# Attention pairs of a fused kernel: the last score tile and the denominators in the bank of the one-chunk values, and three pieces of work elsewhere in the queues

## The chip, the cores and the metric

The kernel runs on one core of a Trainium2 chip. The metric is the device time of one execution in microseconds (us), here the median of three runs. The core's engines are TensorE (PE, with its weight loads shown as PEld), VectorE (DVE), ScalarE (ACT), GpSimd (POOL) and SyncE (SP), which issues most DMA transfers. Each engine works through its own queue in the order in which the program was written; engines wait for each other by semaphores. PSUM, into which TensorE writes, has eight banks of 512 fp32 columns on 128 partitions.

## What is computed

Three layers in a row: attention with rotary embedding over 4 batches and 8 heads of 576 tokens with 64 dimensions, a dense block `h - tanh(h)`, and a block that sends chosen tokens to one of 8 experts. The change lies in the attention:

```python
q_rot, k_rot = (rotate(q), rotate(k))
scores = scale * np.matmul(q_rot, k_rot.transpose(0, 1, 3, 2))
scores = scores - np.max(scores, axis=-1, keepdims=True)
attn = np.exp(scores)
attn = attn / (np.sum(attn, axis=-1, keepdims=True) + 1e-09)
return np.matmul(attn, v).astype(np.float32)
```

## The kernel before

**Work.** The 32 heads are taken as 16 pairs (`p`). A head's 576 rows are four and a half chunks of 128; the two halves left over share one mixed chunk, so that a pair has 9 chunks, numbered 0 to 8, chunk 4 being the mixed one. Every number is fp32; a matmul of two fp32 operands is three matmuls of rounded high and low parts (`high`, `low`).

**Steps.** The loop in `attention` goes over pairs and, in each, over five steps `s` (`STEPS`): steps 0 to 3 take two chunks, step 4 the mixed chunk alone. A step writes the scores of its chunks into score banks ("pair" tiles, two of two banks each; `scores`, L229), has VectorE take the negated row max (`nm`, L234), has ScalarE take the exponent with the row sum beside it (`exponent`, L247), and has TensorE transpose finished exponents in tiles of 128x128 (`transpose`, L261). A pair has 41 tiles. Chunk `c` owns the tiles from `FIRST[c]` on; tiles 36 to 40 are those of the mixed chunk. `BEFORE[s]` and `BEHIND[s]` list the tiles transposed ahead of and behind a step's scores; those in `BEHIND[0]`, 36 to 40, belong to the pair that has just ended and are done in step 0 of the next one.

**Banks of the tiles.** Four tiles fill a bank. Banks 0 and 1 are taken in turn (`cnt["b"]`), so that a pair takes eleven: ten full ones and one for tile 40, into which the transposed denominators (9 rows of 128 columns) go as well. `evacuate` copies full banks to the tile `eT` in SBUF (L271), on ScalarE, but for the bank of tiles 36 to 39, which VectorE copies. Banks 2 and 3 hold the values: bank 2 those of the eight whole chunks, bank 3, in its first 64 columns, those of the mixed chunk (`values`, `pav`). The score tiles take the other four.

**Step 0 of pair p.** In order: `evacuate` (tiles 28 to 35 of p - 1, two ScalarE copies); `denominators(p - 1)`, a ScalarE copy of 9 sums per row with 1e-9 added (L275) and a VectorE reciprocal (L276); `scores`; the transposes of tiles 36 to 40 and of the reciprocals (L263); the copies of the two banks, VectorE and ScalarE; `spread(p - 1)`, a VectorE copy of the transposed reciprocals (`sT`, L281), its transfer to DRAM (L282) and back to all partitions (`rb`, L284 and L285); the exponents; the rotations of pair p + 2 on GpSimd (L201 to L203); and the last part of the values of p - 2 (`AV[3]`, L303). Step 1 ends the pair p - 2 (`finish`, L325 and L328, VectorE), which multiplies the values of both banks by the spread reciprocals, and then starts the values of p - 1 in both.

**Weights on the side.** A 64-bit weight block per pair is decoded to fp32 in four parts (`w_decode`): part 0 on ScalarE (L350), parts 1 to 3 on VectorE (L352 and L354; L357; L362). They stand behind the scores and exponents of the steps in `W_AT` = (1, 2, 4), in pair 0 of `W_AT0` = (3, 4, 4). Part 3 ends a block: most are stored to DRAM at the next step 0 (`w_store`), but in pairs 13 and 14 the block stays, and ScalarE casts its high part (L126) and GpSimd takes the low part (L127) at once.

**After the loop** come the stores, the rest of the values and the first matmuls of the MoE stage (`g1(0, ...)`, L531), between whose halves `last_transposes` ends the last pair.

**Waits within a bank.** The semaphores come from a framework that orders any two accesses of different engines to one PSUM tile, and so to one bank.

Of the kernel before, what the change touches and what calls it, by code (L numbers as in the profile page):

```python
# [19 lines left out]
P = 128  # L20
# [3 lines left out]
NP = 16  # L24
# [20 lines left out]
W_AT, W_AT0 = (1, 2, 4), (3, 4, 4)  # L45
# [5 lines left out]
BEHIND = range(36, 41), range(4, 8), range(12, 18), range(20, 26), range(28, 36)  # L51
# [28 lines left out]
class Chain:  # L80
# [90 lines left out]
    def attention(self, ctx):  # L171
        nc, tc = self.nc, self.tc
        a1 = ctx.enter_context(tc.tile_pool(name="a1", bufs=1))

        def tile_(shape, tag, dt=F32, bufs=1):
            return a1.tile(shape, dt, tag=tag, name=tag, bufs=bufs)
# [36 lines left out]

        cnt = {"b": 0}

        def scores(p, cs):

            (qh, ql), (kh, kl) = parts[p, 0], parts[p, 1]
            banks = [self.pair_bank() for _ in cs]
            for i in range(2):
                for n, (q, k) in enumerate(((qh, kh), (ql, kh), (qh, kl))):
                    for c, sc in zip(cs, banks):
                        r = slice(0, P) if c == 4 else half[c // 5]
                        a = P * (c % 5)
                        x = 288 * i + (0 if c in (1, 3, 6, 8) else 64)
                        nc.tensor.matmul(sc[:, i, :288], q[r, a:a + P], k[r, x:x + 288], start=n == 0, stop=n == 2)  # L229
            if p not in st:  # L230
                st[p] = {"sums": tile_([P, 9], "sums", bufs=2), "eT": tile_([P, 44 * P], "eT", bufs=2)}
            for c, sc in zip(cs, banks):
                nm = tile_([P, 1], "nm", bufs=4)
                nc.vector.tensor_reduce(out=nm, in_=sc[:, :, :288], axis=AX.XY, op=ALU.max, negate=True)  # L234
                st[p][c] = (sc, nm)
# [15 lines left out]
        def transpose(p, tiles):  # L251

            d = st[p]
            for L in tiles:
                c = max((a, c) for c, a in enumerate(FIRST) if a <= L)[1]
                j, odd = L - FIRST[c], c in (1, 3, 6, 8)
                if L % 4 == 0:
                    d["pt"] = self.bank(cnt["b"] % 2)
                    cnt["b"] += 1
                x = 512 * odd + j * P  # L260
                nc.tensor.transpose(d["pt"][:, (L % 4) * P:(L % 4 + 1) * P], d["e", c][:, x:x + P], self.ident)  # L261
                if L == 40:
                    nc.tensor.transpose(d["pt"][:9, P:2 * P], d["s2"], self.ident)  # L263
                if L % 4 == 3 or L == 40:
                    full.append((d, d["pt"], L))

        def evacuate(f=nc.scalar.copy, n=None):
            for _ in range(len(full) if n is None else n):
                d, pt, L = full.pop(0)
                a, n = (L - L % 4) * P, (L % 4 + 1) * P  # L270
                f(d["eT"][:, a:a + n], pt[:, :n])  # L271

        def denominators(p):
            s2 = st[p]["s2"] = tile_([P, 9], "s2", bufs=2)
            nc.scalar.activation(s2, st[p]["sums"], AF.Copy, bias=1e-9)  # L275
            nc.vector.reciprocal(s2, s2)  # L276

        def spread(p):
            d = st[p]
            sT = tile_([9, P], "sT", bufs=2)  # L280
            nc.vector.tensor_copy(sT, d["pt"][:9, P:2 * P])  # L281
            nc.sync.dma_start(self.rd[p].rearrange("(c t) -> c t", t=P), sT)  # L282
            rb = d["rb"] = self.k([P, 1024], "wraw", bufs=4)[:, :SK] if p + 1 == NP else tile_([P, SK], "rb", bufs=2)
            nc.sync.dma_start(rb[:64, 64:], self.rd[p, :S].partition_broadcast(64))  # L284
            nc.sync.dma_start(rb[64:, :S], self.rd[p, S:].partition_broadcast(64))  # L285

        def values(p):
            d = st[p]
# [7 lines left out]
                a = 4 * h + j  # L296
                return eT[:, a:a + 36].rearrange("k (a n) q -> k a n q", a=2)[:, :, 0:10 + h:9 + h]

            d["pav"] = (self.bank(2), self.bank(3))

            def main(j):
                for h in range(2):
# [111 lines left out]
        for p in range(NP):  # L414
            for s, cs in enumerate(STEPS):
                if s:
                    transpose(p, BEFORE[s])
                evacuate()
                for i in range(2):
                    if s == CAST_AT[i] and p + 1 < NP:  # L420
                        high(p + 1, i)
                if s == (MAGNITUDE_AT if p else W_AT0[0]):
                    w_decode(p, 0)
                if s == 0 and p:
                    denominators(p - 1)
                if s == 1 and p > 1:
                    finish(p - 2)
                scores(p, cs)
                if s:
                    transpose(p, BEHIND[s])  # L430
                elif p:
                    transpose(p - 1, BEHIND[0])
                    evacuate(nc.vector.tensor_copy, 1)
                    evacuate()
                    spread(p - 1)
                for c in cs:
                    exponent(p, c)
                if p == 0 and s == 0:
# [10 lines left out]
                    for h in range(2):  # L449
                        nc.sync.dma_start(vt[half[h], 4 + h], self.vr[p])  # L450
                for i, at in enumerate(W_AT if p else W_AT0):
                    if s == at:
                        w_decode(p, i + 1)
                if s == W_LOAD_AT:
                    w_store()
# [18 lines left out]
        def last_transposes():  # L474
            denominators(NP - 1)
            evacuate()
            transpose(NP - 1, BEHIND[0])
            evacuate()
            spread(NP - 1)

        self.g1(0, last_transposes)
        self.load_w(9)
# [1 line left out]
        for f in values(NP - 1):  # L484
            f()
# [866 lines left out]
```

## Time and profile before

| | us |
|---|---|
| median of three runs | 896.14 |
| the runs | 895.75, 901.04, 896.14 |
| the profiled execution | 895.3 |
| its span, first to last instruction | 893.5 |

The mean granted clock of TensorE in the profiled execution is 0.983 of full speed. A row of the timeline has the start in us from the span's start, the duration in us, engine, line, operation, output<-inputs with shapes, and how many instructions were merged; in square brackets stands how long the engine was idle before it, and what ended that. Idle times under some tens of ns are not shown.

### The profile page before, as it was taken

To read this page: it belongs to the slowest core of one execution; us is meant where nothing else is said; L and a number is where in the kernel's file an instruction comes from. 1 tells how busy PE (TensorE), PEld (TensorE's weight loads), DVE (VectorE), ACT (ScalarE), POOL (GpSimd) and SP (SyncE) were. 2 spreads that over 40 slices of the span, in tenths; PEclk is the share of its full clock that TensorE was granted. 3 is DMA by queue.
4 is the path that set the end of the run, shared out by engine and by line. 5 is a ranking of instruction groups with operands and counts; after the bars stand their busy time and mean duration, and the time that the engine had idled before them with its cause. 6 is when DMAs were issued, how large, how long until landed. Compare 5 with 4: busy or idle time off the path is not lost. (4 is left out here: it accounts for less than half of the span.)

```text
span 893.5 us, 14400 instructions
## 1 busy us (share of the span) xinstructions
PE 834.4 (93%) x5224; PEld 678.4 (76%) x5224; DVE 686.7 (77%) x1248; ACT 520.7 (58%) x1064; POOL 297.1 (33%) x190
## 2 busy tenths in 40 slices
PE   4699989999999999999999999999999998899996
PEld 4465656665665579998998898998998887788874
DVE  3788888888887679987877877787887975776571
ACT  3677778877777767554454454544444464355550
POOL 6964575657651100000300200110110246435452
PEclk8799999999999999999999999999999999999998
DMA  8257655675564163230020011002001056497760
GB/s 302 82 194 238 226 194 205 231 256 183 180 220 145 42 246 119 82 106 1 1 91 16 1 61 46 2 14 95 1 1 72 24 201 201 123 335 259 238 218 11
DMA packets 53866, 117.55 MB, mean 132 GB/s; under 512 B 7547, under 2 KB 13195, under 8 KB 53792
## 3 DMA queue, kind: packets, MB, share of 16 engines
q1 hardware_dynamic: 51152, 111.06, 36.4%
q0 software_dynamic: 2640, 5.55, 1.8%
q8 instruction: 42, 0.69, 0.3%
q14 instruction: 32, 0.26, 0.1%
HBM read 92.84 MB, written 24.79 MB: 132 GB/s over the span
## 5 line engine op out<-in xcount | busy, mean ns | idle before, releaser
L234 DVE TENSOR_REDUCE nm<-pair 128x1 f32<-128x576 f32 x144 | 102.0, 744 | 43.7 <-PE pair L229 42.7
L531 PE MATMUL pair<-xh,wh 128*128 128x384 f32 x384 | 131.9, 343 | 0.9 <-DVE ct L587 0.9
L531 PE MATMUL pair<-xh,wl 128*128 128x384 f32 x384 | 129.4, 337 | 0.0
L531 PE MATMUL pair<-xl,wh 128*128 128x384 f32 x384 | 129.2, 336 | 0.0
L596 ACT CAST gh<-cq 128x384 fp32r<-128x384 f32 x96 | 46.7, 512 | 129.6 <-PE bank L545 75.8
L545 PE MATMUL bank<-wh,gl 128*128 128x512 f32 x288 | 112.6, 391 | 0.0
L545 PE MATMUL bank<-wl,gh 128*128 128x512 f32 x288 | 112.5, 391 | 0.0
L545 PE MATMUL bank<-wh,gh 128*128 128x512 f32 x288 | 112.3, 390 | 0.0
L261 PE MATMUL bank<-ident,e 128*128 128x128 f32 x576 | 91.9, 288 | 20.2 <-ACT e L247 11.8
L247 ACT ACTIVATE e<-pair,nm 128x576 f32<-128x576 f32 x128 | 93.7, 738 | 28.8 <-DVE nm L234 27.0
L127 POOL TENSOR_TENSOR xl<-wraw,xh 128x768 fp32r<-128x768 f32 x12 | 23.1, 1924 | 262.1 <-ACT xh L126 262.0
L229 PE MATMUL pair<-k,q 64*128 64x288 f32 (+1 forms) x864 | 97.1, 318 | 12.4 <-ACT emix L247 9.5
L261 PEld LDWEIGHTS bank<-ident,e 128*128 128x128 f32 x576 | 63.1, 143 | 56.2 <-ACT e L247 39.1
L271 ACT COPY eT<-bank 128x512 f32<-128x512 f32 (+1 forms) x161 | 83.3, 555 | 24.6 <-PE bank L263 15.0
L229 PEld LDWEIGHTS pair<-k,q 64*128 64x128 f32 (+1 forms) x864 | 73.1, 190 | 28.8 <-ACT emix L247 12.9
L580 ACT ACTIVATE cu<-pair 128x384 f32<-128x384 f32 x96 | 47.1, 490 | 49.8 <-PE pair L531 49.7
L531 PEld LDWEIGHTS pair<-xh,wh 128*128 128x128 f32 x384 | 72.1, 188 | 4.7 <-issue 1.6
L531 PEld LDWEIGHTS pair<-xl,wh 128*128 128x128 f32 x384 | 72.2, 188 | 1.2
L531 PEld LDWEIGHTS pair<-xh,wl 128*128 128x128 f32 x384 | 72.1, 188 | 0.0
L303 PE MATMUL bank<-eT,vt 128*64 128x512 f32 x256 | 69.8, 624 | 0.0
L594 DVE COPY_PREDICATED cq<-ck,ct 128x384 f32<-128x384 uint8 x96 | 65.1, 678 | 2.8
L927 ACT CAST wh<-wraw 128x1024 fp32r<-128x1024 f32 x56 | 56.6, 1050 | 16.2 <-DMA wraw<-w 16.0
(216 smaller groups left out, 1826.0 us busy)
## 6 DMA issues: line engine op xcount, KB each, us to landing
wraw<-w SPq DMA_DIRECT2D x56, 512.0 KB
raw<-qs SPq DMA_DIRECT2D x15, 640.0 KB
raw<-ks SPq DMA_DIRECT2D x15, 640.0 KB
wu<-w_in SPq DMA_DIRECT2D x8, 1024.0 KB
wu<-w_out SPq DMA_DIRECT2D x8, 1024.0 KB
w_d<-wb SPq DMA_DIRECT2D x14, 512.0 KB
wraw<-w_d SPq DMA_DIRECT2D x14, 512.0 KB
wraw<-xf_d SPq DMA_DIRECT2D x12, 384.0 KB
```

The source lines that it names most:

```text
L229: nc.tensor.matmul(sc[:, i, :288], q[r, a:a + P], k[r, x:x + 288], start=n == 0, stop=n == 2)
L234: nc.vector.tensor_reduce(out=nm, in_=sc[:, :, :288], axis=AX.XY, op=ALU.max, negate=True)
L247: nc.scalar.activation(o.rearrange("p (h s) -> p h s", h=2), sc[:, :, :288], AF.Exp, bias=nm, accum_out=st[p]["sums"][:, c:c + 1])
L261: nc.tensor.transpose(d["pt"][:, (L % 4) * P:(L % 4 + 1) * P], d["e", c][:, x:x + P], self.ident)
L271: f(d["eT"][:, a:a + n], pt[:, :n])
L303: nc.tensor.matmul(d["pav"][0][half[h]], vt[:, j, half[h]], of_head(h, j), start=j == 0, stop=j == 3)
L531: self.nc.tensor.matmul(h[f], a[:, k, fs], b[:, k], start=n == 0, stop=n == 11)
L545: self.nc.tensor.matmul(self.acc[g][t], a[:, f, ts], b[:, f], start=(p == 0 and f == 0 and i == 0), stop=(p == 7 and f == 1 and i == 2))
L580: nc.scalar.activation(u, x, AF.Square)
L594: V.copy_predicated(q, mk, th)
L596: nc.scalar.copy(gh, q)
L927: self.nc.scalar.copy(h, self.eraw[l, q])
```

## The change

Bank 3 becomes one tile, `odds`, for all of the attention: columns 0 to 63 hold the mixed chunk's values as before, columns 128 to 255 tile 40, columns 256 to 383 the transposed denominators. Tile 40 takes no bank of the two alternating ones any more. `last_tiles` transposes the last five tiles, has VectorE copy tiles 36 to 39, calls `spread`, and has VectorE copy tile 40; in the last pair too, where ScalarE made both copies before. `denominators` goes ahead of `evacuate` in step 0. The decode parts that stand at step 4 (part 3; in pair 0 parts 2 and 3) go from behind the step's exponents to ahead of its scores.

```diff
@@ attention @@
         cnt = {"b": 0}
 
+        odds = self.bank(3)
+
@@ transpose @@
-                if L % 4 == 0:
+                if L == 40:
+                    d["pt"] = odds[:, P:2 * P]
+                elif L % 4 == 0:
                     d["pt"] = self.bank(cnt["b"] % 2)
                     cnt["b"] += 1
...
                 if L == 40:
-                    nc.tensor.transpose(d["pt"][:9, P:2 * P], d["s2"], self.ident)
+                    nc.tensor.transpose(odds[:9, 2 * P:3 * P], d["s2"], self.ident)
@@ spread @@
-            nc.vector.tensor_copy(sT, d["pt"][:9, P:2 * P])
+            nc.vector.tensor_copy(sT, odds[:9, 2 * P:3 * P])
...
+        def last_tiles(p):
+
+            transpose(p, BEHIND[0])
+            evacuate(nc.vector.tensor_copy, 1)
+            spread(p)
+            evacuate(nc.vector.tensor_copy, 1)
+
@@ values @@
-            d["pav"] = (self.bank(2), self.bank(3))
+            d["pav"] = (self.bank(2), odds)
@@ the loop over pairs and steps @@
                 if s:
                     transpose(p, BEFORE[s])
+                if s == 0 and p:
+                    denominators(p - 1)
                 evacuate()
...
                 if s == (MAGNITUDE_AT if p else W_AT0[0]):
                     w_decode(p, 0)
-                if s == 0 and p:
-                    denominators(p - 1)
                 if s == 1 and p > 1:
                     finish(p - 2)
+                for i, at in enumerate(W_AT if p else W_AT0):
+                    if s == at == 4:
+                        w_decode(p, i + 1)
                 scores(p, cs)
                 if s:
                     transpose(p, BEHIND[s])
                 elif p:
-                    transpose(p - 1, BEHIND[0])
-                    evacuate(nc.vector.tensor_copy, 1)
-                    evacuate()
-                    spread(p - 1)
+                    last_tiles(p - 1)
...
                 for i, at in enumerate(W_AT if p else W_AT0):
-                    if s == at:
+                    if s == at != 4:
                         w_decode(p, i + 1)
@@ last_transposes @@
             denominators(NP - 1)
             evacuate()
-            transpose(NP - 1, BEHIND[0])
-            evacuate()
-            spread(NP - 1)
+            last_tiles(NP - 1)
```

## Rows read from the trace of the kernel before

**Rows 1.** The page, busy us of each engine (share of the span), instructions

```profile
PE 834.4 (93%) x5224; PEld 678.4 (76%) x5224; DVE 686.7 (77%) x1248; ACT 520.7 (58%) x1064; POOL 297.1 (33%) x190
```

**Rows 2.** Table of stretches, 200 to 250 us: busy us by engine, PEclk, DMA share, GB/s

```profile
200.00:250.00 50.00, 46.29 (x387) 29.77 (x386) 44.31 (x59) 38.53 (x88) 33.70 (x19) 1.00 0.58 196
```

**Rows 3.** Waits of PE, 60 to 300 us: total us, times, longest

```profile
PE bank L261 <- DVE eT L271: 6.4, 13, 0.7
```

**Rows 4.** Timeline, 160 to 182 us, the end of pair 7

```profile
164.15 0.76 DVE L234 TENSOR_REDUCE nm<-pair 128x1 f32<-128x576 f32 x1 [1.38 <-PE pair L229]
...
164.94 0.74 ACT L247 ACTIVATE emix<-pair,nm 128x576 f32<-128x576 f32 x1 [0.28 <-DVE nm L234]
...
165.67 1.07 ACT L271 COPY eT<-bank 128x512 f32<-128x512 f32 x2
...
166.62 0.23 ACT L275 ACTIVATE s<-sums 128x9 f32<-128x9 f32 x1
...
166.81 0.77 PE L261 MATMUL bank<-ident,emix 128*128 128x128 f32 x5
...
167.61 1.08 PE L303 MATMUL bank<-eT,vt 128*64 128x512 f32 x4
167.72 0.27 ACT L271 COPY eT<-bank 128x128 f32<-128x128 f32 x1 [0.87 <-PE bank L263]
167.88 0.75 ACT L247 ACTIVATE e<-pair,nm 128x576 f32<-128x576 f32 x1
...
168.28 0.68 DVE L271 COPY eT<-bank 128x512 f32<-128x512 f32 x1
...
168.88 0.27 DVE L281 COPY sT<-bank 9x128 f32<-9x128 f32 x1
...
169.11 0.63 PE L261 MATMUL bank<-ident,e 128*128 128x128 f32 x4 [0.42 <-DVE eT L271]
...
170.77 1.42 DVE L234 TENSOR_REDUCE nm<-pair 128x1 f32<-128x576 f32 x2 [0.64 <-PE pair L229]
```

**Rows 5.** One line's instructions (ns min/median/max), and a group of POOL, 60 to 300 us

```profile
L362 DVE SCALAR_TENSOR_TENSOR wb<-wu,wb x16: 1214/1756/2580, 36.4 to 311.7; 128x1024 uint32<-128x1024 uint32 x16
...
L201 POOL TENSOR_TENSOR t<-raw,csq 128x640 f32<-128x640 f32 x11 | 20.8, 1895 | 68.5 <-DMA raw<-qs 44.4 <-DVE nm L234 18.0 <-DVE k L212 6.1
```

**Rows 6.** Timeline, 30 to 46 us, the end of pair 0

```profile
34.44 1.88 DVE L357 SCALAR_TENSOR_TENSOR wb<-wu,wb 128x1024 uint32<-128x1024 uint32 x1
...
35.44 1.80 PE L229 MATMUL pair<-k,q 64*128 64x288 f32 x11 [3.29 <-ACT emix L247]
...
36.36 2.46 DVE L362 SCALAR_TENSOR_TENSOR wb<-wu,wb 128x1024 uint32<-128x1024 uint32 x1
...
40.96 1.09 PE L261 MATMUL bank<-ident,e 128*128 128x128 f32 x4 [1.58 <-DVE eT L271]
```

**Rows 7.** Timeline, 53 to 62 us, the end of pair 1

```profile
55.10 2.12 POOL L202 TENSOR_TENSOR t<-raw,csq 128x640 f32<-128x640 f32 x1
...
55.97 0.76 DVE L234 TENSOR_REDUCE nm<-pair 128x1 f32<-128x576 f32 x1
56.64 1.67 DVE L362 SCALAR_TENSOR_TENSOR wb<-wu,wb 128x1024 uint32<-128x1024 uint32 x1
```

**Rows 8.** Timeline, 127 to 130 us, the end of pair 5

```profile
127.68 1.56 POOL L201 TENSOR_TENSOR t<-raw,csq 128x640 f32<-128x640 f32 x1 [6.12 <-DVE k L212]
```

**Rows 9.** Timeline, 272 to 283 us, the end of pair 13

```profile
273.67 0.74 ACT L247 ACTIVATE emix<-pair,nm 128x576 f32<-128x576 f32 x1 [1.00 <-DVE nm L234]
...
274.81 1.05 ACT L126 CAST wh<-wb 128x1024 fp32r<-128x1024 f32 x1 [0.30 <-DVE wb L362]
...
281.47 1.42 DVE L234 TENSOR_REDUCE nm<-pair 128x1 f32<-128x576 f32 x2 [0.85 <-PE pair L229]
```

**Rows 10.** Timeline, 291 to 302 us, the end of pair 14

```profile
293.03 0.74 ACT L247 ACTIVATE emix<-pair,nm 128x576 f32<-128x576 f32 x1 [0.90 <-DVE nm L234]
...
300.20 1.42 DVE L234 TENSOR_REDUCE nm<-pair 128x1 f32<-128x576 f32 x2 [0.64 <-PE pair L229]
```

## The prediction

> **What bounds the kernel now.** I read the page first: TensorE is busy 93% of the span, no other engine over 77% [rows 1]. Then the table of stretches, since the change lies in the attention stage alone (about 16 to 316 us, 16 pairs of some 18 us): in 50 us there TensorE is busy 46.3, VectorE 44.3, ScalarE 38.5 [rows 2]. So TensorE bounds this stage with small holes, and only what closes or opens a hole counts. Then who TensorE waits for between 60 and 300 us: 6.4 us, 13 times, for VectorE's copy at L271 [rows 3]. Last the timeline around the end of a pair, which I call a boundary and number by the pair that ends; number 7 stands for eight that look alike (1, 2, 3, 4, 6, 7, 9, 12) [rows 4]. There the reader is to see: the max of step 4 (164.15, VectorE idle 1.38 before it), the exponent of the mixed chunk (164.94), which frees the score bank that TensorE needs for the next pair; the transposes of the last five tiles (166.81); the values matmuls (167.61 to 168.69); and then 0.42 us of nothing until 169.11, because the first four tiles of the next pair go into the bank whose 512 columns VectorE has just copied out (ends 168.96).
>
> **The change, part by part.**
>
> *Tile 40 and the denominators move to bank 3.* A pair now takes ten banks of the two alternating ones in place of eleven. So the first tiles of the next pair no longer follow tiles 36 to 39 in one bank but tiles 32 to 35, whose copy on ScalarE is over by 166.74 (165.67 + 1.07, plus the 0.23 below) [rows 4]. The wait of 6.4 us in 13 boundaries goes [rows 3]. What is late next: the values matmuls end at 168.69, and the exponent of the next pair's first chunk ends at 168.62 now (167.88 + 0.74); to the 0.15 us that a release takes (168.96 to 169.11) that would bind at 168.77. But this exponent starts late today because ScalarE's copy of tile 40 (167.72, held 0.87 us for TensorE) stands ahead of it; the max it needs ends about 167.69. Without the copy it starts about 0.15 us earlier and ends at 168.47. So TensorE goes on right at 168.70: 0.40 of the 0.42 is gained, 6.2 us in all.
> Bank 3 still holds the unread mixed values of the pair before while tile 40 is written beside them. That TensorE waits for no reader there I take from the order of work: the last reader of bank 3 ran one step 1 earlier, some 17 us before.
>
> *Tile 40's copy moves to VectorE.* The trace has no such copy there. Below: the copy of as many columns on 9 partitions, 0.27 us; above: the 512 columns, 0.68 us [rows 4]. The columns are those of the first, so I take 0.27, that is 0.19 after the overlap of 0.08 that neighbours show (168.28 + 0.68 against 168.88). It lies ahead of step 1's max, which has 0.64 us of idle time before it [rows 4]. TensorE's 0.40 takes from the same idle time: 0.64 - 0.40 - 0.19 leaves 0.05. The cover just holds, at no cost; at 0.68 it would be missed by 0.36 per boundary. The transfer of the denominators is not behind the new copy, since `spread` is called ahead of it. In the last pair both copies go from ScalarE to VectorE, under the matmuls of the first MoE block: nothing.
>
> *Denominators ahead of the copies at step 0.* ScalarE's 0.23 us come before two copies that start at 165.67 [rows 4]. The first then ends near 166.45, and with 0.15 for the release its bank is free at 166.60, before TensorE asks at 166.81. Cost nothing, with 0.2 us of cover. VectorE's reciprocal comes earlier, which is worth something only where L362 made it late; that is left out of the sum.
>
> *The last decode step (L362) goes ahead of the scores of step 4.* On VectorE it now stands in front of the max at 164.15, with that max, the exponent of the mixed chunk and all of TensorE's next scores queued behind. It takes 1.21 to 2.58 us [rows 5]. The cover is the idle 1.38 us, so 1.21 fits and 2.58 would not. The long ones are those in which GpSimd's rotations (two operands from SBUF) run too: in boundary 1 GpSimd's row that starts at 55.10 ends at 57.22, and L362, begun at 56.64, ends at 58.31, 1.09 after it [rows 7]. GpSimd mostly begins its rotations when a transfer lands (44.4 us of its waits [rows 5]), and in all of boundaries 2 to 12 that is later than VectorE's coming free; boundary 5 is the earliest, at 127.68, 1.24 us ahead of its max [rows 8]. Then L362 comes first, takes 1.21 and delays nothing. After the change this landing comes about 0.2 us later against the max, as pairs get 0.40 shorter and its issue only 0.2 earlier.
> The Trainium skill ("SBUF — State Buffer", Who interferes with whom) says that a VectorE instruction with two SBUF inputs and a GpSimd one that reads SBUF exclude each other, and that whoever issues first has the shared ports for the whole instruction. The 1.09 us after GpSimd's end agrees [rows 7]. By it the order of issue alone decides what this move costs; that is the second rival.
>
> Two boundaries lack the cover. *Boundary 0:* VectorE is full (the max follows a long decode step), and two decode steps, L357 and L362, go ahead of the max: 1.88 + 2.46 less overlaps = 4.2 us [rows 6]. TensorE's scores, resumed at 35.44, then resume at 39.65; in 1.80 us they end at 41.45; max and exponent of the first chunk (0.7 and 0.74, with gaps) end near 42.95, and the next transposes start at 43.1 in place of 40.96. Cost 2.1: half of the delay comes back, since today VectorE does the same decode work before the next max. *Boundary 1:* the max starts at 55.97 with no idle time before it. L362 put there runs against GpSimd's row that ends at 57.22, and then 1.09 more, to 58.3 [rows 7]: the max is 2.2 late. Were GpSimd out of the way it would be 1.1 (1.21 less the overlap). I take 2.2, the row.
>
> *Boundaries 13 and 14* have a ScalarE cast of 1.05 us behind L362 (L126), which holds the two copies and so TensorE's transposes, then the denominators and the next max [rows 9]. It now comes before the exponent, in ScalarE's idle time (1.00), with 0.06 and 0.17 us left over. From the mixed exponent to step 1's max, boundary 7 takes 170.77 - 164.94 = 5.83; less 0.40 is 5.43 [rows 4]. Boundary 13 takes 281.47 - 273.67 = 7.80, boundary 14 300.20 - 293.03 = 7.17 [rows 9, 10]. They gain 7.80 - 5.49 = 2.3 and 7.17 - 5.60 = 1.6, of which 0.7 (boundary 14's wait for VectorE) is in the 6.2 already.
>
> *Sum.* Gains 6.2 + 2.3 + 0.9 = 9.4; costs 2.1 + 2.2 = 4.3; net 5.1 us. The profiled execution took 895.3 (span 893.5 and 1.8 around it): 890.2. The median of the runs shown, 896.14, lies 0.8 above it: 891.0, which I give. TensorE goes on from attention to the MoE stage without a hole, so the gain stays to the end.
>
> **Rivals.**
>
> *VectorE takes over as the bound of step 1.* The cover there is 0.05 us by my count. If the new copy costs up to 0.68, each of 13 boundaries gives back up to 0.36, 4.7 us: 895.7, no change. For it: VectorE is busy 44.3 of 50 [rows 2]. Against: the 0.27 of a copy with as many columns.
>
> *GpSimd gets the ports first (the slower side).* If at most boundaries a rotation is under way when VectorE reaches L362, the max waits for the rest of that rotation. The point: GpSimd's start before VectorE comes free, 1.38 us ahead of the max, where the trace shows it no earlier than 1.24 ahead [rows 8]. A rotation is 1.56 us alone [rows 8], so L362 ends 1.21 + (0 to 1.56) after, and the max is up to 1.4 late. Over the 11 boundaries 2 to 12 that is up to 15 us: 891.0 + 15 = 906. At half, 898.5. For it: boundary 1. Against: the landings come too late in the other eleven.
>
> *The relief spreads.* L362 out of GpSimd's way ends the mutual blocking: 16 of them have a median of 1.76 against 1.21 alone [rows 5]. GpSimd then ends each rotation up to 1 us sooner and hinders the decode steps of step 1 less. If 0.3 us of that reaches TensorE in 13 boundaries, 3.9 more: 887.1. That boundary 0 or 1 costs only half belongs here too.
>
> **How the numbers follow.** Forecast 0.62, VectorE as the bound 0.16, GpSimd first 0.10, spreading relief 0.12. About 1%, or 9 us, is what can be told from no change. Faster by more than that needs under 887.2: the last case and the forecast's lower edge, 0.17. Slower by more needs over 905: the upper end of GpSimd first, 0.06 with what I overlook. The rest, 0.77, lies within. The range: the spreading case with a cheap boundary 0 reaches 885.5; the forecast with both copy and boundaries at their dear ends (+4.7, and boundary 0 a whole 4.2) reaches 898, which takes in half of the GpSimd case.
>
> **What would show it.** In the profile after: the wait of L261's matmuls for VectorE's L271 gone; 128x128 copies on VectorE of about 0.27; step 1's max with idle time near 0.05; most L362 at 1.21, with the max of step 4 not over 0.1 late behind them in boundaries 2 to 14; boundaries 0 and 1 late by 2 us each; the idle time before L261 of boundaries 13 and 14 gone. The forecast is wrong if the first transposes of a pair find another wait of 0.4, or if most L362 take over 1.5.

## The result, and the profile after

The kernel after takes 889.6 us (median of six runs, 887.6 to 889.9), the kernel before beside it 895.9 (six runs): a ratio of 0.9913, with a 95% interval of 0.9892 to 0.9934 (the medians alone give 0.9929). That is 6.3 us between the medians. The profiled execution took 887.63 us (span 885.8), that of before 895.3 (893.5): 7.7 less. The forecast was 891.0, 4.9 to 5.1 less by its two bases.

The page's engine row, to be held against [rows 1]:

```profile
PE 833.2 (94%) x5224; PEld 679.5 (77%) x5224; DVE 691.3 (78%) x1265; ACT 519.3 (59%) x1047; POOL 290.5 (33%) x190
```

VectorE has 17 instructions more and ScalarE 17 fewer: the copy of tile 40, once a pair, and one more copy of the last pair. TensorE has the same work in a shorter span. The same 50 us stretch as in [rows 2] (busy us of PE, PEld, DVE, ACT, POOL, each with its count; then PEclk, DMA share, GB/s) shows it:

```profile
200.00:250.00 50.00, 47.76 (x406) 31.20 (x406) 43.61 (x64) 40.22 (x88) 29.80 (x19) 1.00 0.63 212
```

TensorE is busy 47.8 us where it was 46.3. Who it still waits for, 60 to 300 us (total us, times, longest), against [rows 3]:

```profile
PE pair L231 <- ACT emix L249: 6.3, 12, 0.6
PE bank L265 <- ACT e L249: 4.3, 7, 1.1
```

The same two waits in the kernel before:

```profile
PE pair L229 <- ACT emix L247: 5.7, 11, 0.5
PE bank L261 <- ACT e L247: 3.3, 6, 1.0
```

The wait for VectorE's copy, 6.4 us in 13 places, is gone, and no wait of that size has come in its place: the other two grew by 0.6 and 1.0. No reader of bank 3 is among those that TensorE waits for, as the forecast had it.

The end of pair 7 in the timeline, the counterpart of [rows 4]. `nm` is now L236, the exponent L249, the transposes L265, the copies L275, `sT` L285, the values L314, the last decode step L373:

```profile
162.44 1.22 DVE L373 SCALAR_TENSOR_TENSOR wb<-wu,wb 128x1024 uint32<-128x1024 uint32 x1
...
163.90 0.76 DVE L236 TENSOR_REDUCE nm<-pair 128x1 f32<-128x576 f32 x1 [0.23 <-PE pair L231]
...
164.69 0.74 ACT L249 ACTIVATE emix<-pair,nm 128x576 f32<-128x576 f32 x1 [0.27 <-DVE nm L236]
...
167.34 0.74 ACT L249 ACTIVATE e<-pair,nm 128x576 f32<-128x576 f32 x1 [0.61 <-DVE nm L236]
...
167.36 1.08 PE L314 MATMUL bank<-eT,vt 128*64 128x512 f32 x4
167.88 0.68 DVE L275 COPY eT<-bank 128x512 f32<-128x512 f32 x1
...
168.37 0.66 PE L265 MATMUL bank<-ident,e 128*128 128x128 f32 x4
...
168.68 0.27 DVE L275 COPY eT<-bank 128x128 f32<-128x128 f32 x1
...
169.47 0.45 DVE L339 TENSOR_TENSOR rb<-bank,rb 64x64 f32<-64x64 f32 x2
...
170.04 1.42 DVE L236 TENSOR_REDUCE nm<-pair 128x1 f32<-128x576 f32 x2
```

Four things are to be seen. The decode step stands ahead of the max and ends 0.24 us before it starts (162.44 + 1.22 = 163.66), so it delays nothing. The first transposes of the next pair start at 168.37, while VectorE still copies tiles 36 to 39 (167.88 to 168.56): before, they had to wait for the end of that copy. Tile 40 costs VectorE 0.27. And step 1's max starts 0.12 us after the last instruction ahead of it (169.47 + 0.45 = 169.92): the cover that was 0.64 wide is nearly used up. From the mixed exponent to step 1's max it is 170.04 - 164.69 = 5.35, before 5.83. This distance is the measure in all that follows: it lies within one boundary, and what happened earlier in the span doesn't enter it.

All 16 instructions of the last decode step (ns, min/median/max), against [rows 5]:

```profile
L373 DVE SCALAR_TENSOR_TENSOR wb<-wu,wb x16: 1217/1220/2439, 36.7 to 301.9; 128x1024 uint32<-128x1024 uint32 x16
```

The median falls from 1756 to 1220: outside pair 0 it no longer runs against GpSimd. GpSimd gains as well; its first rotation, 1895 ns in the mean before, in the groups of 60 to 300 us after:

```profile
L201 POOL TENSOR_TENSOR t<-raw,csq 128x640 f32<-128x640 f32 x11 | 17.0, 1547 | 71.9 <-DMA raw<-qs 50.3 <-DVE nm L236 14.4 <-DVE wb L373 7.2
```

Boundary 0, against [rows 6] (L368 is the decode step that was L357):

```profile
33.57 1.97 POOL L202 TENSOR_TENSOR t<-raw,csb 128x640 f32<-128x640 f32 x1
34.19 2.43 DVE L368 SCALAR_TENSOR_TENSOR wb<-wu,wb 128x1024 uint32<-128x1024 uint32 x1
35.62 2.39 POOL L203 TENSOR_TENSOR t<-t,t 128x640 f32<-128x640 f32 x1
36.66 2.44 DVE L373 SCALAR_TENSOR_TENSOR wb<-wu,wb 128x1024 uint32<-128x1024 uint32 x1
...
39.02 0.74 DVE L236 TENSOR_REDUCE nm<-pair 128x1 f32<-128x576 f32 x1
...
40.68 1.81 PE L231 MATMUL pair<-k,q 64*128 64x288 f32 x11 [8.21 <-ACT emix L249]
...
43.97 1.12 PE L265 MATMUL bank<-ident,e 128*128 128x128 f32 x4
```

TensorE stands still for 8.21 us (3.29 before), and its next transposes start at 43.97 in place of 40.96: 3.0 late, where the forecast had 2.1. Of these 0.3 are older than the boundary: step 3's max of this pair starts at 27.43, before at 27.12. Each decode step ends 1.08 or 1.09 us after the rotation that it meets (35.54 to 36.62, 38.01 to 39.10). L357 did likewise in the kernel before, where it ends at 36.32 [rows 6] and the rotation at 35.25:

```profile
33.27 1.98 POOL L202 TENSOR_TENSOR t<-raw,csb 128x640 f32<-128x640 f32 x1
```

Boundary 1, against [rows 7], was forecast 2.2 late:

```profile
57.24 1.22 DVE L373 SCALAR_TENSOR_TENSOR wb<-wu,wb 128x1024 uint32<-128x1024 uint32 x1
...
57.49 2.38 POOL L201 TENSOR_TENSOR t<-raw,csq 128x640 f32<-128x640 f32 x1 [9.24 <-DMA raw<-qs]
...
58.59 0.76 DVE L236 TENSOR_REDUCE nm<-pair 128x1 f32<-128x576 f32 x1
```

Here VectorE came first, by 0.25 us, and GpSimd waited. The max comes no later against the pair's start than before. Boundary 13, against [rows 9]:

```profile
269.81 1.05 ACT L126 CAST wh<-wb 128x1024 fp32r<-128x1024 f32 x1
...
270.81 0.74 ACT L249 ACTIVATE emix<-pair,nm 128x576 f32<-128x576 f32 x1
...
276.18 1.42 DVE L236 TENSOR_REDUCE nm<-pair 128x1 f32<-128x576 f32 x2
```

ScalarE's cast is over as the mixed exponent begins, and the distance is 5.37 where it was 7.80. Not all of these 2.4 us are the cast's own. For a part of this boundary TensorE was granted the lower of its two clock levels (PEclk 0.50, 1.2 GHz) in the kernel before:

```profile
276.80:280.20 3.40, 3.40 (x13) 1.29 (x11) 2.90 (x7) 1.86 (x7) 1.49 (x1) 0.50 0.01 1
```

Its four values matmuls took 1.97 us there, against 1.08 in boundary 7, and the four transposes behind them 0.99 against 0.63: some 1.2 us by these rows, an estimate. In the kernel after the granted clock is 1.00 through boundary 13.

### The profile page after: what moved, and what is told of

Read it like the earlier page. It is cut to its first block, busy times and chain, and to the rows that moved or that the text cites. A ratio compares the mean times of both kernels' runs of the same rounds, so it can differ in the third digit from the quotient of the medians.

```text
span 885.8 us, 14370 instructions
## 1 busy us (share of the span) xinstructions
PE 833.2 (94%) x5224; PEld 679.5 (77%) x5224; DVE 691.3 (78%) x1265; ACT 519.3 (59%) x1047; POOL 290.5 (33%) x190
## 5 line engine op out<-in xcount | busy, mean ns | idle before, releaser
L236 DVE TENSOR_REDUCE nm<-pair 128x1 f32<-128x576 f32 x144 | 103.0, 752 | 29.8 <-PE pair L231 25.9
L249 ACT ACTIVATE e<-pair,nm 128x576 f32<-128x576 f32 x128 | 93.8, 738 | 38.5 <-DVE nm L236 36.9
L265 PE MATMUL bank<-ident,e 128*128 128x128 f32 x576 | 92.2, 288 | 12.1 <-ACT e L249 11.8
L231 PEld LDWEIGHTS pair<-k,q 64*128 64x128 f32 (+1 forms) x864 | 73.7, 192 | 33.1 <-ACT emix L249 17.9
L265 PEld LDWEIGHTS bank<-ident,e 128*128 128x128 f32 x576 | 62.8, 143 | 47.1 <-ACT e L249 30.4
L275 ACT COPY eT<-bank 128x512 f32<-128x512 f32 x144 | 78.5, 587 | 4.3 <-PE bank L265 4.3
L314 PE MATMUL bank<-eT,vt 128*64 128x512 f32 x256 | 69.4, 621 | 0.0
L941 POOL TENSOR_TENSOR wl<-wraw,wh 128x1024 fp32r<-128x1024 f32 x25 | 60.6, 2450 | 19.8 <-ACT wh L936 19.6
```

Of the source, the lines that this page charges most:

```text
L249: nc.scalar.activation(o.rearrange("p (h s) -> p h s", h=2), sc[:, :, :288], AF.Exp, bias=nm, accum_out=st[p]["sums"][:, c:c + 1])
L314: nc.tensor.matmul(d["pav"][0][half[h]], vt[:, j, half[h]], of_head(h, j), start=j == 0, stop=j == 3)
L941: eng.tensor_tensor(out=lo, in0=self.eraw.pop((l, q)), in1=h.bitcast(F32), op=ALU.subtract)
```

## The experiments

A table of what the profiled executions show comes first, in us against the kernel before. "Pair 0" is how much later pair 1's step 1 begins (its max), and the row below it counts the same from the max of step 3 of pair 0 on; the other rows are the change of the distance from the mixed exponent to step 1's max. "Ordinary" is the median of boundaries 2, 3, 4, 6, 7, 9 and 12.

| | forecast | after | bank alone | decode alone | denominators alone |
|---|---|---|---|---|---|
| pair 0 | +2.1 | +3.0 | +1.7 | +5.9 | +0.5 |
| of it from step 3 on | +2.1 | +2.7 | -0.1 | +4.2 | 0.0 |
| ordinary boundary | -0.40 | -0.46 | -0.41 | 0.00 | -0.15 |
| boundary 13 | -2.3 | -2.4 | -1.0 | -2.0 | -1.3 |
| boundary 14 | -1.6 | -1.8 | +0.8 | -1.4 | +0.7 |
| boundaries 1 to 14 in sum | -9.4 | -10.6 | -5.7 | -3.0 | -1.5 |

The row of pair 0 holds also what differs from one execution to the next: with the bank alone, which changes nothing in pair 0 ahead of its last tiles, it is 1.7 all the same, and all of that is there by step 3. The row below it is free of this: a second profile of the kernel after, which comes below, has 4.0 in the one row and 2.8 in the other.

**One part alone, three times.** The bank part is the kernel before with `odds`, tile 40, the denominators' columns and `last_tiles`. The decode part is the kernel before with this:

```diff
+                for i, at in enumerate(W_AT if p else W_AT0):
+                    if s == at == 4:
+                        w_decode(p, i + 1)
                 scores(p, cs)
...
-                    if s == at:
+                    if s == at != 4:
                         w_decode(p, i + 1)
```

The third is the kernel before with `denominators(p - 1)` ahead of `evacuate()`. What was expected:

> The kernel before with the bank part alone: tile 40 and the denominators in bank 3, tile 40 copied by VectorE; the denominators and the decode steps stay where they were. Theory (the parts add up): TensorE's wait for VectorE's copy at the end of a pair is gone, 0.40 to 0.47 us in each of 13 boundaries, some 6 us, so about 890 against 896. Rival (the copy ahead of step 1's max takes back what the bank gives, or the gain needs the decode step out of the way as well): 894 or more.

> The kernel before with the decode step of step 4 ahead of the scores, nothing else. Theory: boundary 0 loses about 3 us, boundaries 13 and 14 gain 1.9 and 1.2, the four boundaries with a long L362 gain 0.8 together: net about +0 us, 895 to 897. Every L362 but those of pair 0 takes 1.22 us. Rival (the relief of GpSimd is where the unforecast part of the gain comes from): 892 or less.

> The kernel before with the denominators ahead of the two copies at step 0, nothing else. Theory: 0.1 us earlier max in the ordinary boundaries and 0.4 to 0.7 us in boundaries 13 and 14: 894 to 896, not to be told from no change. Rival (ScalarE's two copies, 0.23 us later, hold the transposes of tiles 36 to 39): 899, 0.2 us per boundary.

Measured beside one another: bank 892.9 us, ratio 0.9950 (0.9920 to 0.9979); decode 895.4, 0.9973 (0.9952 to 0.9995); denominators 895.6, 0.9980 (0.9954 to 1.0006), which is not to be told from no change. In the sum that is -0.97%, the whole change -0.87%; the intervals allow that the parts add up. The bank's time lies between its theory (890) and its rival (894), the other two are as their theories had them. The bank has the largest part, though by the times alone its interval overlaps with the others, and it alone ends the wait for VectorE: ordinary boundaries gain 0.41 with it, nothing with the decode step and 0.15 with the denominators.

Boundaries 13 and 14 get most of their 2.4 and 1.8 from the decode step, 2.0 and 1.4 with it alone. That boundary 14 grows by 0.8 and 0.7 with the bank or the denominators alone goes with TensorE's clock: the stretch at the lower level, which the kernel before has in boundary 13, lies in boundary 14 there. First the bank, then the denominators:

```profile
290.70:294.10 3.40, 3.40 (x11) 1.28 (x12) 3.15 (x8) 1.71 (x5) 0.95 (x1) 0.50 0.01 1
```

```profile
298.20:301.60 3.40, 3.40 (x12) 1.30 (x11) 2.06 (x4) 1.81 (x6) 1.45 (x1) 0.50 0.01 4
```

So the two boundaries are better taken together: -0.2 with the bank, -0.6 with the denominators, -3.3 with the decode step, -4.2 with all. The three profiles in which the cast stands behind the mixed exponent have such a stretch in one of the two; the nine in which the decode step stands ahead of the scores there have none.

What the decode step gives it pays again at boundaries 0 and 1, in its profile (the slowest of its ten runs) more than that: 5.9 in pair 0, and 2.1 and 1.1 in the steps and the distance of pair 1. One point of its theory failed: L362 was to be short outside pair 0, and took 2.58 at boundaries 1 and 5, where GpSimd came first.

**Boundary 0 without the move.** The change, but pair 0 keeps its decode steps behind:

```diff
-                    if s == at == 4:
+                    if s == at == 4 and p >= 1:
                         w_decode(p, i + 1)
...
-                    if s == at != 4:
+                    if s == at and not (s == 4 and p >= 1):
                         w_decode(p, i + 1)
```

> The changed kernel, but in pair 0 the two decode steps stay behind the exponent of step 4. Theory A (the 3 us of boundary 0 are a pure loss): 886.5 against 889.6, and the max of step 4 in pair 1 is not late. Theory B (the delay of boundary 0 is what kept GpSimd out of boundary 1): boundary 1's max comes 1 to 2.3 us late, with L362 over 1.6 us there, and the whole is 888 to 890.

Measured: 888.0 us, ratio 0.9913 (0.9884 to 0.9943), the same as the whole change, as theory B had it. Boundary 0 lost its cost (-0.1 from step 3 on), and boundary 1 took on another. The timeline of this kernel, at the end of pair 1:

```profile
54.95 1.55 POOL L201 TENSOR_TENSOR t<-raw,csq 128x640 f32<-128x640 f32 x1 [6.48 <-DMA raw<-qs]
...
56.45 2.12 POOL L202 TENSOR_TENSOR t<-raw,csq 128x640 f32<-128x640 f32 x1
...
57.10 2.55 DVE L373 SCALAR_TENSOR_TENSOR wb<-wu,wb 128x1024 uint32<-128x1024 uint32 x1
...
59.58 0.75 DVE L236 TENSOR_REDUCE nm<-pair 128x1 f32<-128x576 f32 x1
60.36 0.74 ACT L249 ACTIVATE emix<-pair,nm 128x576 f32<-128x576 f32 x1 [3.38 <-DVE nm L236]
```

This time the transfer landed 2.15 us ahead of VectorE. GpSimd was rotating (L202, 56.45 to 58.57), L373 took 2.55, and against pair 1's start the max came 2.4 us later than in the kernel before: the forecast's 2.2. And then the boundary lost still more: its distance grew by 1.05 where the others shrink by 0.46. The stretches of the same kernel show what went with it (after the busy times come PEclk, DMA share, GB/s):

```profile
58.00:61.20 3.20, 0.25 (x1) 0.03 (x1) 2.32 (x2) 0.83 (x2) 3.12 (x3) 1.00 0.00 0
61.20:63.00 1.80, 1.76 (x12) 1.49 (x13) 0.42 (x2) 1.17 (x3) 1.80 (x2) 0.54 0.00 0
63.00:65.00 2.00, 2.00 (x8) 1.26 (x10) 2.00 (x5) 1.41 (x4) 1.92 (x2) 0.56 0.01 4
```

TensorE was busy 0.25 of 3.2 us, and in the 3.8 us that followed it was granted 0.54 and 0.56 of its clock, the lower of its two levels for most of the time; from 65 on it was 1.00 again. By the distances this hole cost itself and 1.05 + 0.46 = 1.5 us behind it, so that boundary 1 cost 2.4 + 1.5 = 3.9. In the two other profiles in which GpSimd came first there with the move, the decode part alone and one that follows, it is 3.3 and 3.4, and the clock fell behind the hole in both.

**Boundaries 0 and 1 without the move**, and the kernel after once more beside it. The edit is the last one with `p >= 2`.

> The changed kernel, but in pairs 0 and 1 the decode steps of step 4 stay behind its exponent. Theory (boundary 0 loses 3 us by the move, and either it or boundary 1 pays, since GpSimd's rotations run at boundary 1 when boundary 0 is not late): both losses go, some 3 us under the changed kernel, about 886.5. Rival (the time is set by the decode step 1 against GpSimd, which gives back what a boundary gains): within 1 us of the changed kernel.

> The changed kernel once more, for a second profile. Theory (the order of GpSimd's first rotation and the decode step at boundary 1 is a close race): the median stays at 889 to 890; if the rotation comes first this time, boundary 1 shows an L362 over 1.6 us and a profiled time 1.5 to 2.5 us above that of the first profile; if the decode step comes first, it takes 1.22 and the profiled time is within 1 us of the first.

Measured: 888.6 us, ratio 0.9906 (0.9870 to 0.9942), and 891.2 for the kernel after, ratio 0.9936 (0.9918 to 0.9955): 2.6 us apart, near the 3 of the theory, with intervals that overlap. The 886.5 were not reached, since the kernel after itself took 1 to 2 us more than the 889 to 890 expected of it. In the trace of the version without the move, step 1 of pair 1 starts 0.24 earlier than in the kernel before and the maxes of steps 4 are on time. The second profile of the kernel after, the fastest of its ten runs and 1.2 us above the first, had VectorE first at boundary 1 again. So by the times the move costs some 2.6 us in pairs 0 and 1 together, and the traces put 2.7 and 2.8 at boundary 0.

**Tile 40's copy back on ScalarE**, ahead of `spread`:

```diff
             transpose(p, BEHIND[0])
             evacuate(nc.vector.tensor_copy, 1)
+            evacuate()
             spread(p)
-            evacuate(nc.vector.tensor_copy, 1)
```

> The changed kernel, but ScalarE copies tile 40, ahead of the spread, as before. Theory: the first exponent of a pair starts 0.15 us later behind that copy, and TensorE's first transposes wait for it by 0.1 us: +1 us, hardly to be told from the changed kernel; VectorE's idle time before step 1's max is 0.2 longer. Rival (VectorE was already the bound of step 1): 1 to 2 us faster than the changed kernel.

Measured: 894.2 us, ratio 0.9971 (0.9949 to 0.9994), 3.0 us more than the kernel after beside it, where 1 was expected. Ordinary boundaries gain 0.30 in place of 0.46, as the exponent of the next pair stands behind the copy again. In the traces boundaries 2 to 14 give 2.1 us less than in the kernel after, of the 3.0. The rival, that VectorE would be better off without the copy, falls. Its profile paid at boundary 1 (a max 2.0 late, a distance 1.1 longer), though boundary 0 was about as late as in the kernel after (from step 3 on, step 4's max was 4.6 late, there 4.9 and 5.3). This contradicts an explanation that I had held until then, that the delay at boundary 0 by itself keeps GpSimd's transfer behind VectorE at boundary 1. What differs is TensorE's clock behind boundary 0's hole. First the kernel after (the execution measured beside this one), then the one with ScalarE's copy:

```profile
46.00:48.00 2.00, 2.00 (x17) 1.51 (x17) 0.21 (x2) 1.54 (x2) 1.92 (x2) 0.70 0.01 2
48.00:50.00 2.00, 2.00 (x29) 1.19 (x28) 1.97 (x4) 1.49 (x5) 0.08 (x1) 1.00 0.61 181
```

```profile
46.00:48.00 2.00, 1.44 (x6) 1.12 (x8) 0.08 (x1) 1.51 (x5) 1.92 (x2) 0.50 0.01 2
48.00:50.00 2.00, 2.00 (x15) 1.72 (x14) 0.55 (x1) 1.33 (x2) 0.23 (x1) 0.50 0.53 135
```

The query transfer was issued at 49.47 in the first and 49.71 in the second, and GpSimd began at 58.98 and 58.93, some 9 us later in both. But VectorE reached L373 at 57.25 in the first and at 61.08 in the second, where pair 1's first steps had run at the lower clock. So VectorE came second. Of the five profiles that have the move in both pairs, three had VectorE first (by 2.4, 1.7 and 0.25 us) and two had GpSimd first (by 2.15 each: this one and the decode part alone). Put in the order in which the clock rose, between 44 and 46, 46 and 48, 48 and 50, 50 and 52, 52 and 54 us, they stand in just this order. What sets the moment at which the clock rises, no run here shows.

**Tile 40 copied three times**, to use up the cover ahead of step 1's max:

```diff
+            more = full[0]
             spread(p)
             evacuate(nc.vector.tensor_copy, 1)
+            for _ in range(2):
+                full.append(more)
+                evacuate(nc.vector.tensor_copy, 1)
```

> The changed kernel with tile 40 copied three times by VectorE. Theory (the cover before step 1's max is 0.13 us): two more copies of 0.19 leave the max 0.25 late in each of 14 boundaries, +3.5 us against the changed kernel, and the max has no idle time before it. Rival (there is other slack behind that max): no difference.

Measured: 892.2 us, ratio 0.9954 (0.9933 to 0.9975). VectorE in the timeline, the end of pair 7 (L343 is the last instruction of `finish`):

```profile
169.53 0.92 DVE L275 COPY eT<-bank 128x128 f32<-128x128 f32 x3
...
170.96 0.45 DVE L343 TENSOR_TENSOR rb<-bank,rb 64x64 f32<-64x64 f32 x2
171.44 0.76 DVE L236 TENSOR_REDUCE nm<-pair 128x1 f32<-128x576 f32 x1
```

The max now follows on VectorE's heels (171.41 to 171.44), and the distance is 0.08 longer than before the change, 0.54 longer than after it: VectorE bounds this stretch. The added copies took (0.92 - 0.27) / 2 = 0.33 each, not the 0.19 of the theory: copies of the same tile to the same place don't overlap here, where neighbours that write elsewhere follow after 0.20. So the cover was real, and it was thin. Yet the time rose only 1.0 us over that of the kernel after beside it, not by the 3.5 expected or by 14 times 0.54: a boundary's distance is not by itself a price in time. In the traces part of it comes back: without the boundaries, pairs 2 to 14 take 2.6 us less than before in sum here, and 1.0 more in the kernel after. Beside this stands that the two decode steps of step 1 take 35.9 us in these pairs, and 39.4 in the kernel after: with the later step 1 more of them miss GpSimd's rotations. That this is the cause no run shows by itself.

**Where a version could go that beats both.** Two edits came from the rows: the decode steps that run against GpSimd in step 1 (L363 and L365, 0.69 us alone and up to 2.06 against GpSimd) could meet it less if the query transfer were issued earlier, or if they stood elsewhere. Both together, each alone, on top of the version that spares pairs 0 and 1:

```diff
-W_AT, W_AT0 = (1, 2, 4), (3, 4, 4)
+W_AT, W_AT0 = (1, 1, 2), (3, 4, 4)
...
+                if s == 0 and p < NP - 3:
+                    load(p + 3)
                 if s == 0 and p:
                     denominators(p - 1)
...
-                if s == LOAD_AT and p < NP - 3:
-                    load(p + 3)
```

> The kernel with pairs 0 and 1 as before (decode behind the exponent there), the transfers of q and k for pair p + 3 issued at the start of step 0 instead of its end, and the decode steps at 1, 1 and 2 instead of 1, 2 and 4. Theory (what still bounds a pair is decode part 1 of step 1 running against GpSimd's rotations, which hold the max of step 2 back by about 1 us in each of 11 pairs): GpSimd starts some 4 us sooner, part 1 takes 1.4 in place of 2 to 4 us, the max of step 2 finds idle time before it: 8 to 12 us under the kernel with pairs 0 and 1 put back, 877 to 881. Rival (the transfers land no sooner, or GpSimd waits for something else): 887 to 892.

> As the run with the transfers moved and the decode steps at 1, 1 and 2, but with the transfers left at the end of step 0. Theory (GpSimd's phase decides): the longer decode at step 1 runs against the rotations and holds the max of step 2 back by a further 1 to 1.5 us in each of 11 pairs: 895 to 905. Rival (the place of the decode steps decides, not GpSimd's phase): 885 or less.

> The kernel with pairs 0 and 1 as before and the transfers issued at the start of step 0, the decode steps at 1, 2 and 4. Theory: GpSimd is now at work when VectorE reaches the decode step ahead of the max of step 4, which takes 1.8 us or more and makes that max about 1 us late (the slower rival of the prediction, brought about on purpose), while part 1 of step 1 gets free of it by about as much: 885 to 893. Rival (the transfers land no sooner): every decode step of step 4 still 1.22 and 888 to 889.

Measured: both 894.4 us, ratio 0.9971 (0.9955 to 0.9987), dearer than either expectation; the decode steps alone 907.8, 1.0127 (1.0108 to 1.0146), dearer than either too; the loads alone 916.6, 1.0237 (1.0215 to 1.0260), where 885 to 893 was expected. All three are misses, and the last is the most telling one. The loads let GpSimd start before VectorE reaches L373, which is the forecast's second rival brought about. The end of pair 3 in its timeline:

```profile
91.11 2.00 POOL L203 TENSOR_TENSOR t<-t,t 128x640 f32<-128x640 f32 x1
...
91.64 2.56 DVE L373 SCALAR_TENSOR_TENSOR wb<-wu,wb 128x1024 uint32<-128x1024 uint32 x1
...
94.12 0.74 DVE L236 TENSOR_REDUCE nm<-pair 128x1 f32<-128x576 f32 x1
...
95.78 1.80 PE L231 MATMUL pair<-k,q 64*128 64x288 f32 x11 [2.78 <-ACT emix L249]
```

TensorE waits 2.78 us, and its eleven score matmuls take 1.80 where twelve took 1.06 (169.67, boundary 7 of the kernel before): the lower clock again.

```profile
95.80:98.00 2.20, 2.20 (x13) 1.92 (x14) 0.82 (x2) 1.13 (x3) 2.12 (x2) 0.50 0.00 0
```

Against the kernel after, nine of the boundaries 2 to 12 come 1.0 to 2.1 late at the max and lose 1.4 to 2.9 behind it, some 3 us each. In just these nine L373 took 2.56 and the clock fell; in boundaries 7, 9, 13 and 14 it took 1.22, the clock stayed at 1.00, and nothing was lost.

With both edits the ordinary pairs took 17.1 us each, where they take 17.1 to 17.9 in the kernel after, but pairs 8, 10, 13 and 14 lost 1.6 to 3.4 each: the first two hold GpSimd's split of the MoE input, the other two the cast behind the decode. In pairs 10 and 14, which lost most, the clock fell as well. The last version mends these four:

```diff
-W_AT, W_AT0 = (1, 1, 2), (3, 4, 4)
+W_AT, W_AT0, W_AT13 = (1, 1, 2), (3, 4, 4), (1, 2, 4)
...
-X_SPLIT = (7, 3), (9, 3)
+X_SPLIT = (8, 0), (10, 0)
...
-                for i, at in enumerate(W_AT if p else W_AT0):
+                for i, at in enumerate(W_AT0 if p == 0 else W_AT if p < 13 else W_AT13):
```

The last line stands at both places of the loop.

> The run with the transfers at the start of step 0 and the decode steps at 1, 1 and 2, with the four pairs mended that lost there by its trace: pairs 8 and 10 (GpSimd's splits of the MoE input come after the rotation, in step 0 of pairs 8 and 10, instead of ahead of it) and pairs 13 and 14 (decode steps at 1, 2 and 4 again, the last ahead of the scores). Theory (all that was lost there came from these four, 2.2, 3.4, 1.6 and 3.3 us by the trace): 10 us under that run's 894.4, about 884, and under the kernel with pairs 0 and 1 put back (888.6), since the other pairs take 17.1 us instead of 17.6. Rival (something else gives the gain back, as the step from 889 to 894 came without warning): 889 or more.

Measured: 882.3 us (879.7 to 886.0), ratio 0.9825 (0.9801 to 0.9848): faster than both kernels, by 15.8 us against the kernel before that ran beside it (898.0), and near the 884 of the theory. In its profiled execution, 886.0 and the longest of the five, attention ends 13.4 us earlier than before. TensorE is busy 48.5 us in the stretch of [rows 2], where it was 46.3 and 47.8. Its waits from 60 to 295 us:

```profile
PE pair L231 <- ACT emix L249: 7.3, 14, 0.6
```

And the timeline, where GpSimd's start now hangs on VectorE itself:

```profile
151.49 0.69 DVE L363 TENSOR_SCALAR wb<-wb 128x1024 f32<-128x1024 f32 x1
...
156.15 1.22 DVE L373 SCALAR_TENSOR_TENSOR wb<-wu,wb 128x1024 uint32<-128x1024 uint32 x1
...
156.31 2.46 POOL L201 TENSOR_TENSOR t<-raw,csq 128x640 f32<-128x640 f32 x1 [6.40 <-DVE q L212]
```

From pair 2 on the decode steps take what they take alone or nearly so (L363 0.69 to 0.78), and the rotation, released by L212 in all of the eleven pairs that begin one after 60 us, waits its turn behind L373.

## Why the prediction was right, and where not

**The bank: right.** 0.40 was forecast for a boundary, 0.41 came with the bank alone and 0.46 with all; nothing else became late there. The rest is the denominators' place (0.15 alone). VectorE's reciprocal used to stand ahead of step 0's maxes, and with it all that follows on VectorE came 0.15 later; now it runs at 165.80, and the first of these maxes starts 1.85 us after the mixed exponent in place of 2.07. The forecast had left this out of its sum.

**The cover ahead of step 1: right, by little.** 0.05 was forecast to be left of 0.64. With the bank alone 0.03 was, in boundary 7, and 0.12 with all, thanks to the denominators. Two more copies took it and made VectorE the bound, so the first rival was near: it needed 0.12 us more of VectorE. What it would have cost was less than its price: the time rose 1.0 us where the distances rose 0.54 each.

**The decode step, boundaries 2 to 14: right.** L373 took 1.22 in 15 of 16 places, the step-4 max was not late behind it, and 13 and 14 gained 2.4 and 1.8 against 2.3 and 1.6. But the 2.3 came out of a row, 7.80, that held some 1.2 us of the lower clock, which the working puts down to the cast with the rest. It came true because in the kernel after the clock does not fall there; the working didn't know of it, so this part of the match is luck.

**Boundary 0: mis-sized.** The term was 4.2 us of delay, half of which comes back, so a cost of 2.1. From step 3 on the max of step 4 was 4.9 late, and the cost was 2.7 (2.8 in the second profile); with the 0.3 from ahead of the boundary that is the 3.0. The fault is in the 4.2. The working gave L368 the 1.88 that L357 had behind the max, and let it start 0.7 us sooner. But its end hung on GpSimd's rotation, before as after: it started sooner and ended no sooner, taking 2.43. L373 too ended where L362 had, 0.3 later (39.10 and 38.82). The lower clock is not what the term lacked up to here: the scores behind the hole took 1.80 before and 1.81 after, so that the row from which the working took 1.80 already had it. But it lasted longer behind the longer hole, until 48 to 50 in place of 44 to 46, and that bears on the next term. The clock had no term in the sum at all.

**Boundary 1: mis-sized, and only by luck on the cheap side.** The term was 2.2. In the profile after it was nothing (-0.4 against the pair's start), since VectorE reached L373 0.25 us before the transfer landed. Where GpSimd came first, the term was right for the max, 2.0 to 2.4, and lacked what the lower clock cost behind it, 1.1 to 1.5. The prediction took the order of issue from before, as if both would move together; the transfer's start and VectorE's steps moved by different amounts.

**The sum.** In the profiled execution the boundaries 1 to 14 gave 10.6 (forecast 9.4), pair 0 cost 3.0 (2.1), the other steps of pair 1 gave 0.4 (a cost of 2.2), and those of pairs 2 to 14 cost 1.0 (0). That is 10.6 - 3.0 + 0.4 - 1.0 = 7.0 at the end of attention, 5.1 forecast; 0.6 more came after it. So the errors of four terms, 1.2, 0.9, 2.6 and 1.0, partly cancelled. The pairs' own steps differ by up to 1.0 either way. In pairs 8 and 10, which hold GpSimd's split, that is no chance: they are 1.0 longer in all four traces of the change and of the versions that spare pair 0 or pairs 0 and 1. In others it varies, with the decode steps of step 1 at 0.69 to 2.0 as GpSimd happened to run; the last version, which takes this out, gains 6 us more in the attention.

**The rivals.** GpSimd first was priced at up to 1.4 a boundary and 15 us in all; brought about by the earlier loads it cost some 3 a boundary, and the kernel was 20 us slower than the one before. The max was late by 1.0 to 2.1, somewhat more than the price, and the clock behind the hole came on top. In the two profiles of the change itself it holds at none of boundaries 1 to 14. With ScalarE's copy it holds at boundary 1, with the decode step alone at 1 and 5. Boundary 5 is the one that the forecast named as nearest, though what released GpSimd there before was VectorE's L212 and not a landing [rows 8]. The Trainium skill ("SBUF — State Buffer", Who interferes with whom) says that the shared ports are held for a whole instruction by whoever issues first; the rows agree to 0.1 us (91.11 + 2.00 + 1.09 = 94.20 for L373's end in the miss above, by the row 91.64 + 2.56 = 94.20). In every meeting of L373 and a rotation that is shown here the order of issue decided. The relief that spreads is seen on GpSimd (1547 for 1895 ns) but not in the pairs' steps.

## What to carry to other kernels

An instruction moved ahead in an in-order queue is free only while its cover is wider than its longest form, and its longest form comes from whom it meets in the new place; look up both ends of that meeting, the neighbour's queue and the transfer that starts it. Where an order hangs on a transfer's landing, it can change from one execution to the next: tie it to an instruction of the engine that is to come first, as it is in the last version. Price a hole in TensorE with what follows it at the lower clock, not by its length alone. And before a distance read from one trace goes into a sum, look at the granted clock of that stretch.

## What was not expected of the hardware

- A hole of 3 us in TensorE, at boundary 1 with pair 0 spared, cost 1.5 us more behind it (granted clock 0.54 and 0.56 for 3.8 us). The Trainium skill ("TensorE: Matmul & The Clock Gate", Part 1: The HAM clock gate) says that the idle array goes to half its clock and gets it back once it has been busy; those rows agree, and the prediction had left it out. No long hole was needed, though: at boundary 13 of the kernel before, TensorE's two waits ahead of the fall at 276.8 are 0.51 and 0.77 us.
- VectorE and GpSimd take turns instruction by instruction: at boundary 0 each of the two decode steps ended 1.08 or 1.09 us after the rotation that it met, and L203, the second of these (35.62 to 38.01), ended 1.39 after the decode step before it (36.62). The one-input decode steps (L363, L365) are held too: 0.69 us alone, 2.05 at 30.17 us in the kernel after.
- Copies of one tile by VectorE to one and the same place follow each other after 0.33 us; copies of two tiles to different places after 0.20 (168.48 to 168.68 in the kernel after). Whether the shared target or the shared source makes the difference, no run separates.
